# Attention over a K/V cache: cache rows of 16 KB, P transposed in 32x32 blocks, PV in diagonal 32x32 tiles

## The chip, the cores and the metric

The kernel runs on one core of a Trainium2 chip. The metric is the device time of one execution in microseconds (us). A profile of one execution comes beside the times: it records what every engine did and when. The engines are PE (TensorE, matmuls; PEld is its weight load, the stationary operand), DVE (VectorE), ACT (ScalarE), POOL (GpSimd) and SP (SyncE, which here issues the transfers from memory).

## The reference: what is computed

One attention block for 32 sequences (B) with 4 new tokens each, against a cache of 2048 positions. There are 32 query heads and 4 heads in the cache, so 8 query heads share one cache head g. All tensors are bf16.

```python
q = (x @ wq).reshape(B, 4, 32, 128).transpose(0, 2, 1, 3)      # x: [32, 4, 1024], wq: [1024, 4096]
k = repeat(k_cache, 8, axis=1)                                  # k_cache, v_cache: [32, 4, 2048, 128]
v = repeat(v_cache, 8, axis=1)
scores = einsum("bhqd,bhkd->bhqk", q, k) * 128 ** -0.5
p = softmax(scores, axis=-1)
o = einsum("bhqk,bhkd->bhqd", p, v)
out = o.transpose(0, 2, 1, 3).reshape(B, 4, 4096) @ wo          # wo: [4096, 1024]
```

The 8 query heads of one cache head times 4 tokens are 32 rows of scores. Four cache heads give 128 rows, so one sequence ("batch" below) fills the 128 partitions.

## The kernel before, in words

**Stages.** x is transposed on PE, Q^T is projected from wq (four loads of 2 MB, L209 to L229), then 32 batches run one after the other, and a last stage multiplies all 128 tokens by wo (L313 to L336, 64 matmuls of 512 columns at L318).

**Loads.** SP issues everything in one order: wq, K of three batches ahead, then V and K in turn, then wo. One load is 2 MB and takes one of nine slots of SBUF. A load waits until the slot's last user has read it (`freed`). K and V arrive as `g (p t) d -> p g (t d)` with p = 128 (L149): a partition gets 16 neighbouring cache positions of each of the four heads, which are four pieces of 4 KB.

**One batch on PE (L281 to L311, in program order).** `qk(i)`: 16 matmuls, QK^T into the four PSUM banks of `ps_s`, four 32-column tiles side by side (L285). `pv(i-1)`: 64 matmuls with a block of V (128x128) as the stationary operand and 32 columns of P^T moving (L267); they sum up O^T in `ps_o`. `kt_fill(i+2, f)`, f = 0 to 7: eight transposes each of K into a PSUM bank (L240). `tr_fill(i, f)`, f = 0 to 3: four matmuls each (L256) that transpose P with a diagonal matrix of 1/sum on the other side, so P^T comes out normalised.

**The ring.** K^T and P^T fills share four PSUM banks (`ps_a`, `ps_b`, `ps_c`, `ps_o`) in turn, and a fill waits until the bank's last fill was copied out (`ring_waits`). DVE and ACT share these copies: of the eight K^T copies ACT does f = 4, 6, 7 (`consumer`).

**The other engines per batch.** DVE: the maximum of each row (L379), the negated and scaled maximum (L380), the copy of O^T to `oT_sb` (L368), K^T copies (L353), 1/sum (L388), the diagonal matrix (L389), two P^T copies (L353). ACT: exp with the sum of each row (L408), then three K^T copies and two P^T copies (L355). Each engine takes its instructions in the order in which the program lists them, and waits where an instruction's semaphore is not there yet.

Of the kernel before, what the change touches and what calls it, by code (L numbers as in the profile page):

```python
# [54 lines left out]
def bass_standalone__gqa_block_cached__sampling_kernel(  # L55
# [17 lines left out]
    G = Hkv  # L73
    scale = float(Dh) ** -0.5
    NSLOT = 9
    SLOT = 8192
    NRING = 4
    KT_FILLS = 2 * G
    TR_FILLS = 4
    AHEAD = 2  # L80
    WQ_LOADS = 4
    WO_LOADS = 4
    HPL = Hq // WO_LOADS

# [5 lines left out]
    with ExitStack() as es:  # L90
        sb = lambda name, shape, dt: es.enter_context(nc.sbuf_tensor(name, shape, dt))
        slots = sb("slots", [128, NSLOT, SLOT], BF16)
        KT_sb = sb("KT_sb", [128, 2, G, Sk], BF16)
        QT_sb = sb("QT_sb", [128, B, Hq, Sq], BF16)
        oT_sb = sb("oT_sb", [128, Hq, NT], BF16)
        pp_sb = sb("pp_sb", [128, 2, Sk], BF16)
        ident = sb("ident", [128, 128], BF16)
        diag = sb("diag", [128, 2, 128], BF16)
# [4 lines left out]
        P_sb = pp_sb[:, 0, :]  # L103
        PT_sb = pp_sb[:, 1, :].rearrange("p (t r) -> p t r", r=128)
        x_sb = pp_sb[:, 0, 0:D]
        xT_sb = pp_sb[:, 0, D:2 * D].rearrange("p (a b) -> p a b", b=128)
        out_sb = pp_sb[:, 1, 0:D]

        ps_s = es.enter_context(nc.psum_tensor("ps_s", [128, Sk], F32))
        ring = [es.enter_context(nc.psum_tensor(f"ps_{c}", [128, 512], F32)) for c in "abco"]  # L110
        ring_f32 = [p[:, :] for p in ring]
        ring_bf16 = [p.bitcast(BF16) for p in ring_f32]
        ps_o = ring_f32[3]
# [3 lines left out]
        for n in ["x", "out"] + [f"slot{i}" for i in range(NSLOT)] + [f"wo{i}" for i in range(4)]:  # L117
            pr.sems[n] = es.enter_context(nc.semaphore(f"s_{n}"))
# [3 lines left out]
        for b in range(AHEAD + 1):  # L122
            stream.append(("k", b))
        for b in range(B):
            stream.append(("v", b))
            if b + AHEAD + 1 < B:
                stream.append(("k", b + AHEAD + 1))
# [13 lines left out]
        pr.load("sp", lambda e: e.dma_start(x_sb, x_flat[:, :]), "x", "x", 16)  # L141
        for n, l in enumerate(stream):
            kind, i = l
            waits = [freed(stream[n - NSLOT])] if n >= NSLOT else []
            s, v = f"slot{n % NSLOT}", 16 * (n // NSLOT + 1)
            if kind == "wq":
                fn = lambda e, l=l, i=i: e.dma_start(slot(l), wq_v[:, i, :])  # L147
            elif kind in "kv":
                src = (k_cache if kind == "k" else v_cache)[i].rearrange("g (p t) d -> p g (t d)", p=128)  # L149
                fn = lambda e, l=l, src=src: e.dma_start(slot(l).rearrange("p (g f) -> p g f", g=G), src)  # L150
            if kind != "wo":
                pr.load("sp", fn, l, s, v, waits)
                continue
            last = i == WO_LOADS - 1
            parts = 4 if last else 1
            per = HPL // parts
            for q in range(parts):
                fn = lambda e, l=l, i=i, q=q, per=per: e.dma_start(
                    slot(l)[:, q * per * D:(q + 1) * per * D].rearrange("p (h n) -> p h n", n=D),
                    wo_v[:, i * HPL + q * per:i * HPL + (q + 1) * per, :],  # L160
                )
                if last:
                    pr.load("sp", fn, ("wo", i, q), f"wo{q}", 16, waits)
                else:
                    pr.load("sp", fn, l, s, v, waits)
# [3 lines left out]

        jobs = [("kt", b, f) for b in range(AHEAD) for f in range(KT_FILLS)]  # L170
        for i in range(B):
            if i + AHEAD < B:
                jobs += [("kt", i + AHEAD, f) for f in range(KT_FILLS)]
            jobs += [("tr", i, f) for f in range(TR_FILLS)]
        job_index = {j: n for n, j in enumerate(jobs)}

        def consumer(job):
            kind, _, f = job
            if kind == "kt":
                return "act" if f in (4, 6, 7) else "dve"  # L180
            return "dve" if f in (0, 2) else "act"

        def ring_waits(job):
            n = job_index[job]
            if n < NRING:
                return [("q_evac", n)]
            w = [("evac",) + jobs[n - NRING]]
            if n % NRING == 3:
                b = job[1] - AHEAD - 1 if job[0] == "kt" else job[1] - 1
                if b >= 0:  # L190
                    w.append(("ot", b))
            return w


        pr.op("pool", lambda e: e.memset(ident[:], 0.0), [], "zero")
        pr.op("pool", lambda e: e.affine_select(
            out=ident[:], in_=ident[:], compare_op=ALU.not_equal, fill=1.0, base=0,
            pattern=[[-1, 128]], channel_multiplier=1), ["zero"], "ident")
# [33 lines left out]
        def kt_fill(b, f):  # L232
            job = ("kt", b, f)
            dst = ring_bf16[job_index[job] % NRING]
            g, half = f // 2, f % 2

            def fn(e):
                for q in range(8):
                    t = half * 8 + q
                    ins = e.transpose(  # L240
                        dst[:, q * 128:(q + 1) * 128],
                        slot(("k", b))[:, (g * NKT + t) * Dh:(g * NKT + t + 1) * Dh],
                        ident[:, :],
                    )
                return ins

            pr.op("pe", fn, [("k", b)] + ring_waits(job), job)

        def tr_fill(b, f):
            job = ("tr", b, f)  # L250
            dst = ring_f32[job_index[job] % NRING]

            def fn(e):
                for q in range(4):
                    t = f * 4 + q
                    ins = e.matmul(dst[:, q * 128:(q + 1) * 128], lhsT=P_sb[:, t * 128:(t + 1) * 128],  # L256
                                   rhs=diag[:, b % 2, :], start=True, stop=True)
                return ins

            pr.op("pe", fn, [("exp", b), ("diag", b)] + ring_waits(job), job)  # L260

        def pv(b):
            def fn(e):
                v = slot(("v", b))
                for g in range(G):
                    for t in range(NKT):
                        ins = e.matmul(  # L267
                            ps_o[:, 32 * g:32 * (g + 1)],
                            lhsT=v[:, (g * NKT + t) * Dh:(g * NKT + t + 1) * Dh],
                            rhs=PT_sb[:, t, 32 * g:32 * (g + 1)],  # L270
                            start=(t == 0),
                            stop=(t == NKT - 1),
                        )
                return ins

            w = [("v", b)] + [("evac", "tr", b, f) for f in range(TR_FILLS)]
            if b > 0:
                w.append(("ot", b - 1))
            pr.op("pe", fn, w, ("pv", b))

        def qk(i):  # L281
            def fn(e):
                for c in range(Sk // 512):
                    for g in range(G):
# [3 lines left out]
                            rhs=KT_sb[:, i % 2, g, c * 512:(c + 1) * 512],  # L288
# [4 lines left out]
                return ins  # L293

            w = [("evac", "kt", i, f) for f in range(KT_FILLS)]
            w += [("q_evac", j) for j in range(NB)] if i == 0 else [("exp", i - 1)]
            pr.op("pe", fn, w, ("qk", i))
# [4 lines left out]
        for i in range(B):  # L302
            qk(i)
            if i >= 1:
                pv(i - 1)
# [165 lines left out]
```

## Time and profile before

| what | value |
|---|---|
| time, median of 3 runs | 389.67 us (389.29 to 390.6) |
| the profiled execution's own time | 388.88 us |
| its span, from the first to the last instruction | 386.9 us |
| busy: PE, PEld, DVE, ACT | 296.0, 246.8, 242.4, 196.6 us |
| moved by DMA | 152.26 MB, mean 393 GB/s |

A row of the profile's groups gives source line, engine, operation, the tensors out<-in, shapes and count; then the busy time, the mean duration of one in ns, the idle time of the engine before it and what ended that. A timeline row gives start, length, engine, line and count of instructions that ran in a row. Matmuls overlap, so the mean of one is longer than the step from one to the next.

### The profile page before, as it was taken

What the parts mean: (1) busy time and instruction counts of PE and PEld (TensorE: products, weight loads), DVE (VectorE), ACT (ScalarE), POOL (GpSimd) and SP (SyncE); (2) the same over time, 40 slices, a digit from 0 to 9 for tenths busy, and PEclk for the clock granted to TensorE, in tenths of its full rate; (3) what the DMA queues carried; (4) which work ended last, traced back from release to release, by engine and by line L of the source; (5) the groups of instructions that cost most, each with busy time, mean ns of one, the idle gap of its engine ahead of it and who ended that gap; (6) DMA issues with size and microseconds to landing.
All of it is one profiled execution on the core that took longest, in us unless ns stands there. A gap on an engine that the chain in (4) does not pass through costs nothing.

```text
span 386.9 us, 11667 instructions
## 1 busy us (share of the span) xinstructions
PE 296.0 (77%) x5448; PEld 246.8 (64%) x5448; DVE 242.4 (63%) x390; ACT 196.6 (51%) x230; POOL 0.7 (0%) x6
## 2 busy tenths in 40 slices
PE   2877787776977977878788869877777787886596
PEld 1777576665766766767667657666666677664542
DVE  0026787775777777758777757877777577774400
ACT  1024766652655565466564635666555564664300
POOL 0000000000000000000000000000000000000000
PEclk9999999998999899889898979999999898997689
DMA  8999999999999999999999999999999999999981
GB/s 327 430 412 410 407 404 407 408 408 409 406 406 409 407 409 410 406 409 407 407 409 409 405 410 410 405 409 408 407 407 407 408 409 407 409 408 359 372 327 56
DMA packets 38912, 152.26 MB, mean 393 GB/s; under 512 B 1232, under 2 KB 1232, under 8 KB 38352
## 3 DMA queue, kind: packets, MB, share of 16 engines
q1 hardware_dynamic: 38864, 151.52, 98.5%
q8 instruction: 42, 0.69, 0.7%
q14 instruction: 6, 0.05, 0.0%
HBM read 151.26 MB, written 0.26 MB: 392 GB/s over the span
## 4 chain that ended last, share of the span: by engine, by line
DMA 87%; PE 7%; ACT 2%; DVE 2%; SPq 1%; issue 0%
DMA slots<-in_k_cache_dram 87%; PE ps_s L318 4%; DVE mx L379 1%; ACT pp_sb L408 1%; PE ps_s L285 1%; ACT KT_sb L355 1%; PE ps_a L240 1%; PE ps_o L267 0%; SPq L147 0%; PE ps_o L256 0%; PE ps_a L256 0%; PE ps_b L240 0%; SPq L150 0%; PE ps_c L256 0%; PE ps_b L256 0%
## 5 line engine op out<-in xcount | busy, mean ns | idle before, releaser
L408 ACT ACTIVATE pp_sb<-ps_s,negmx 128x2048 bf16<-128x2048 f32 x32 | 62.9, 1967 | 93.1 <-DVE negmx L380 93.1
L379 DVE TENSOR_REDUCE mx<-ps_s 128x1 f32<-128x2048 f32 x32 | 73.3, 2292 | 35.3 <-PE ps_s L285 35.3
L240 PE MATMUL ps_a<-ident,slots 128*128 128x128 bf16 x512 | 43.8, 234 | 42.2 <-DMA slots<-in_k_cache_dram 41.3
L240 PEld LDWEIGHTS ps_a<-ident,slots 128*128 128x128 bf16 x512 | 33.7, 105 | 46.1 <-DMA slots<-in_k_cache_dram 44.9
L267 PEld LDWEIGHTS ps_o<-pp_sb,slots 128*128 128x128 bf16 x2048 | 53.5, 96 | 14.6 <-issue 13.7
L267 PE MATMUL ps_o<-pp_sb,slots 128*128 128x32 bf16 x2048 | 56.7, 177 | 0.8 <-ACT pp_sb L355 0.8
L355 ACT ACTIVATE KT_sb<-ps_a 128x1024 bf16<-128x1024 bf16 x32 | 32.6, 1020 | 45.6 <-PE ps_a L240 45.6
L240 PE MATMUL ps_o<-ident,slots 128*128 128x128 bf16 x512 | 42.7, 231 | 7.8 <-DVE KT_sb L353 7.8
L353 DVE COPY KT_sb<-ps_b 128x1024 bf16<-128x1024 bf16 x64 | 43.7, 683 | 5.2 <-PE ps_b L240 5.2
L353 DVE COPY KT_sb<-ps_a 128x1024 bf16<-128x1024 bf16 x32 | 22.1, 689 | 35.0 <-PE ps_a L240 35.0
L240 PE MATMUL ps_c<-ident,slots 128*128 128x128 bf16 x512 | 43.3, 233 | 0.7 <-issue 0.7
L240 PE MATMUL ps_b<-ident,slots 128*128 128x128 bf16 x512 | 43.5, 234 | 0.0
L240 PEld LDWEIGHTS ps_o<-ident,slots 128*128 128x128 bf16 x512 | 33.8, 105 | 11.4 <-DVE KT_sb L353 11.2
L240 PEld LDWEIGHTS ps_c<-ident,slots 128*128 128x128 bf16 x512 | 34.8, 105 | 1.5 <-issue 0.9
L240 PEld LDWEIGHTS ps_b<-ident,slots 128*128 128x128 bf16 x512 | 35.2, 106 | 0.4
L285 PE MATMUL ps_s<-KT_sb,QT_sb 128*32 128x512 bf16 x512 | 34.3, 389 | 0.0
L355 ACT ACTIVATE KT_sb<-ps_c 128x1024 bf16<-128x1024 bf16 x32 | 32.7, 1021 | 1.9 <-PE ps_c L240 1.9
L355 ACT ACTIVATE KT_sb<-ps_o 128x1024 bf16<-128x1024 bf16 x32 | 32.9, 1027 | 0.0
L353 DVE CAST pp_sb<-ps_a 128x512 bf16<-128x512 f32 x32 | 22.1, 692 | 12.8 <-PE ps_a L256 12.8
L256 PE MATMUL ps_o<-diag,pp_sb 128*128 128x128 bf16 x128 | 13.2, 227 | 14.7 <-ACT KT_sb L355 14.7
L353 DVE CAST pp_sb<-ps_c 128x512 bf16<-128x512 f32 x32 | 21.9, 685 | 1.9 <-PE ps_c L256 1.6
L353 DVE COPY KT_sb<-ps_c 128x1024 bf16<-128x1024 bf16 x32 | 21.9, 684 | 1.0 <-PE ps_c L240 1.0
(46 smaller groups left out, 244.7 us busy)
## 6 DMA issues: line engine op xcount, KB each, us to landing
slots<-in_k_cache_dram SPq DMA_DIRECT2D x32, 2048.0 KB, 25.0
slots<-in_v_cache_dram SPq DMA_DIRECT2D x32, 2048.0 KB, 24.2
slots<-in_wq_dram SPq DMA_DIRECT2D x4, 2048.0 KB, 14.9
slots<-in_wo_dram SPq DMA_DIRECT2D x3, 2048.0 KB, 25.6
slots<-in_wo_dram SPq DMA_DIRECT2D x4, 512.0 KB, 12.2
pp_sb<-in_x_dram SPq DMA_DIRECT2D x1, 256.0 KB, 2.7
out_dram<-pp_sb SPq DMA_DIRECT2D x1, 256.0 KB, 2.2
```

The lines of the kernel that those rows point to most:

```text
L240: ins = e.transpose(dst[:, q * 128:(q + 1) * 128], slot(("k", b))[:, (g * NKT + t) * Dh:(g * NKT + t + 1) * Dh], ident[:, :],)
L256: ins = e.matmul(dst[:, q * 128:(q + 1) * 128], lhsT=P_sb[:, t * 128:(t + 1) * 128], rhs=diag[:, b % 2, :], start=True, stop=True)
L267: ins = e.matmul(ps_o[:, 32 * g:32 * (g + 1)], lhsT=v[:, (g * NKT + t) * Dh:(g * NKT + t + 1) * Dh], rhs=PT_sb[:, t, 32 * g:32 * (g + 1)], ...
L285: ins = e.matmul(ps_s[32 * g:32 * (g + 1), c * 512:(c + 1) * 512], lhsT=QT_sb[:, i, REP * g:REP * (g + 1), :], rhs=KT_sb[:, i % 2, g, c * ...
L318: ins = e.matmul(ps_s[:, c * 512:(c + 1) * 512], lhsT=oT_sb[:, h, :], rhs=w[:, h - i * HPL, c * 512:(c + 1) * 512], start=(h == 0), stop=( ...
L353: pr.op("dve", lambda e: e.tensor_copy(dst, src), w, ("evac",) + job)
L355: pr.op("act", lambda e: e.activation(dst, src, ACT.Copy), w, ("evac",) + job)
L379: pr.op("dve", lambda e, i=i: e.tensor_reduce(mx[:, i:i + 1], ps_s[:, :], AX.X, ALU.max), [("qk", i)], ("max", i))
L408: pr.op("act", lambda e, i=i: e.activation(P_sb, ps_s[:, :], ACT.Exp, bias=negmx[:, i:i + 1], scale=scale, accum_out=ssum[:, i:i + 1]), [( ...
```

## The change

The rows that a partition holds are other ones. K and V are now loaded as `g (p t) d -> (g p) (t d)` with p = 32: partition 32g+p holds 64 neighbouring positions of head g, one piece of 16 KB. The rest follows from this layout.

- K^T: transposing one of the 64 blocks gives 32 columns of each of the four heads, so `qk` takes its moving operand from K^T with a step between runs of 32 elements. It waits per pair of fills, in four parts.
- P^T: one DVE instruction transposes all of P in 32x32 blocks, SBUF to SBUF (L378), in place of 16 matmuls, four PSUM copies and the diagonal matrix. P^T has three buffers.
- PV: for each of the 64 positions t, four matmuls, one per head, each on 32 of the array's rows and 32 of its columns (`tile_position` 32g, 32g). P^T is stationary (32x32), V moves (32x128). Head g's sum stands in bank g of the ring, partitions 32g to 32g+31, so PV takes all four ring banks: it waits for the last copy out of each, and the next four fills wait for PV's results to be copied out (`pv`).
- The output: four ACT instructions of 32x128 scale it by 1/sum on the way to `o_sb` (L352), one PE transpose turns it (L247), one ACT copy takes it to `oT_sb` (L359).
- PV runs two batches behind QK (LAG 2, before 1), K is loaded four batches ahead (before 3), there are eight slots (before 9). ACT takes K^T fills 4 to 7, DVE 0 to 3. wo is loaded in 16 parts issued by POOL, after V of batch 30 has landed.

```diff
-    NSLOT = 9
+    NSLOT = 8
+    LAG = 2
...
-                src = (k_cache if kind == "k" else v_cache)[i].rearrange("g (p t) d -> p g (t d)", p=128)
+                src = v_cache[i].rearrange("g (p t) d -> (g p) (t d)", p=KP)
...
-                    pr.load("sp", fn, l, s, v, waits)
+                    pr.load("pool", fetch(part, wo_v[:, h0:h0 + WO_PER, :]), ("wo", i, q), f"wo{i * WO_PARTS + q}", 16, waits + [("v", B - 2)])
...
+        def take(job):
+            bank = turn[0] % NRING
+            turn[0] += 1
+            bank_of[job] = bank
+            before = bank_last[bank]
+            bank_last[bank] = ("evac",) + job
+            return bank, [before]
...
+        def o_fill(b):
+            job = ("o", b)
+            bank, waits = take(job)
+            dst = ring_bf16[bank]
+            pr.op("pe", lambda e: e.transpose(dst[:, 0:128], o_sb[:, b % 2, :], ident[:, :]), [("raw", b)] + waits, job)
+
+        def pv(b):
+            waits = list(bank_last.values())
+            for n in range(NRING):
+                bank_last[n] = ("raw", b)
...
-                for g in range(G):
-                    for t in range(NKT):
+                for t in range(KTOK):
+                    for g in range(G):
                         ins = e.matmul(
-                            ps_o[:, 32 * g:32 * (g + 1)],
-                            lhsT=v[:, (g * NKT + t) * Dh:(g * NKT + t + 1) * Dh],
-                            rhs=PT_sb[:, t, 32 * g:32 * (g + 1)],
+                            pv_bank[g],
+                            lhsT=PT_buf[rows, b % NPT, t, :],
+                            rhs=v[rows, t, :],
...
+                            tile_position=(KP * g, KP * g),
...
+            pr.op("pe", fn, [("v", b), ("pt", b)] + waits, ("pv", b))
...
         for i in range(B):
             qk(i)
-            if i >= 1:
-                pv(i - 1)
+            if i > LAG:
+                o_fill(i - 1 - LAG)
+            if i >= LAG:
+                pv(i - LAG)
             if i + AHEAD < B:
                 for f in range(KT_FILLS):
                     kt_fill(i + AHEAD, f)
-            for f in range(TR_FILLS):
-                tr_fill(i, f)
...
+        def raw_evac(b):
+            for g in range(G):
+                rows = slice(KP * g, KP * (g + 1))
+                w = [("pv", b), ("rinv", b)] + ([("o", b - 2)] if b >= 2 else [])
+                pr.op("act", lambda e, g=g, rows=rows: e.activation(
+                    o_sb[rows, b % 2, :], pv_bank[g], ACT.Copy, scale=rinv[rows, b:b + 1]),
+                    w, ("raw", b) if g == G - 1 else None)
...
+            pr.op("dve", lambda e, i=i: e.transpose(PT_buf[:, i % NPT, :, :].rearrange("p t r -> p (t r)"), P_sb),
+                  [("exp", i)] + ([("pv", i - NPT)] if i >= NPT else []), ("pt", i))
```

The order in which PE gets its instructions, with what the first of each run waits for: one batch before. s_act, s_dve and s_slot0 are the semaphores that ACT, DVE and the load of a slot count up; `pp_sb` holds P and P^T.

```order
L285 MATMUL ps_s<-KT_sb,QT_sb 32x512 x16
L267 MATMUL ps_o<-pp_sb,slots 128x32 [waits s_act,s_dve,s_slot0]
L267 MATMUL ps_o<-pp_sb,slots 128x32 x63
L240 MATMUL ps_a<-ident,slots 128x128 [waits s_slot1]
L240 MATMUL ps_a<-ident,slots 128x128 x7
L240 MATMUL ps_b<-ident,slots 128x128 x8
L240 MATMUL ps_c<-ident,slots 128x128 x8
L240 MATMUL ps_o<-ident,slots 128x128 [waits s_dve]
```

The same place of the changed program; `ps_r` is the whole ring.

```order
L275 MATMUL ps_s<-KT_sb,QT_sb 32x512 [waits s_act]
L275 MATMUL ps_s<-KT_sb,QT_sb 32x512 x15
L247 MATMUL ps_r<-ident,o_sb 128x128 [waits s_act]
L259 MATMUL ps_r<-slots,PT_sb 32x128 [waits s_act,s_slot2]
L259 MATMUL ps_r<-slots,PT_sb 32x128 x255
L233 MATMUL ps_r<-ident,slots 128x128 [waits s_act,s_slot3]
L233 MATMUL ps_r<-ident,slots 128x128 x31
L233 MATMUL ps_r<-ident,slots 128x128 [waits s_dve]
```

The K^T fills behind PV waited for their load alone; now the first of them waits for ACT as well (PV's results copied out), and PV itself waits for ACT's copy of the transposed output, which stands behind ACT's last K^T copy.

ACT's order, one batch before:

```order
L408 ACTIVATE pp_sb,ssum<-ps_s,negmx 128x2048
L355 ACTIVATE KT_sb<-ps_a 128x1024
L355 ACTIVATE KT_sb<-ps_c 128x1024
L355 ACTIVATE KT_sb<-ps_o 128x1024
L355 ACTIVATE pp_sb<-ps_b 128x512
L355 ACTIVATE pp_sb<-ps_o 128x512
```

And now:

```order
L359 ACTIVATE oT_sb<-ps_r 128x32x4
L352 ACTIVATE o_sb<-ps_r,rinv 32x128 x4
L393 ACTIVATE P_sb,ssum<-ps_s,negmx 128x2048
L338 ACTIVATE KT_sb<-ps_r 128x1024 x4
```

ACT's exp stood ahead of the K^T copies and behind nothing of PV; now it stands behind the four scaled copies of PV's result.

234 lines of the change are left out of this document (95 added, 139 removed).

## The prediction

> **What bounds the kernel now.** I read the page first: the span, the chain that ended last, and the bandwidth in 40 slices.
>
> ```profile
> span 386.9 us, 11667 instructions
> ...
> GB/s 327 430 412 410 407 404 407 408 408 409 406 406 409 407 409 410 406 409 407 407 409 409 405 410 410 405 409 408 407 407 407 408 409 407 409 408 359 372 327 56
> ...
> DMA 87%; PE 7%; ACT 2%; DVE 2%; SPq 1%; issue 0%
> ```
>
> The chain is 87% DMA, and the bandwidth stands at 404 to 412 GB/s from the third slice to the 36th: the transfers run without a break while K and V are loaded. A batch is 4.19 MB (two loads of 2.097 MB), which at 408 GB/s takes 10.28 us, and 32 of them 329 us.
>
> Next the waits (us in total, times, the longest): do the engines wait for transfers?
>
> ```profile
> PE ps_a L240 <- DMA slots<-in_k_cache_dram: 41.3, 30, 3.4
> ```
>
> In 30 of the batches PE waits for its next K, 1.4 us each. So PE is ahead of the transfers, by little: what counts is how much serial work the change puts into one batch, set against 10.28 us.
>
> The speed of the transfers by stretch (time, PE, PEld, DVE, ACT, POOL busy, clock, DMA share, GB/s): wq, whose rows are 16 KB already, then K and V in 4 KB, then wo.
>
> ```profile
> 5.00:20.00 15.00, 8.87 (x130) 8.70 (x131) 0.30 (x1) 0.00 (x0) 0.00 (x0) 1.00 0.99 421
> ...
> 200.00:210.00 10.00, 7.66 (x137) 6.64 (x138) 6.61 (x10) 5.06 (x7) 0.00 (x0) 0.83 1.02 408
> ...
> 365.00:375.00 10.00, 8.75 (x95) 4.68 (x93) 0.92 (x2) 0.70 (x2) 0.00 (x0) 0.74 1.00 373
> ```
>
> With 16 KB pieces a batch would take 4.19 MB / 421 = 9.96 us, at the 430 of the second slice 9.75 us. That is the whole gain that the new rows can bring, 0.3 to 0.5 us a batch, and only while transfers are what is waited for.
>
> **The change: one round of a batch.** In the program's order PE runs qk(i), the transpose of O(i-3), pv(i-2), then eight K^T fills. PV now takes all four ring banks. So the round closes on itself: PV waits for the last K^T copies out of the ring (ACT's f = 4 to 7) and for ACT's O copy behind them; the next fills wait for ACT's four scaled copies of PV's result; ACT's exp stands behind those; ACT's K^T copies stand behind exp. Before, PV only needed `ps_o` and ran beside the others' copies. I add up this ring, counted from PV's last matmul. First two durations of ACT, from the groups by shape (busy us, mean ns of one, idle before):
>
> ```profile
> L355 ACT ACTIVATE KT_sb<-ps_c 128x1024 bf16<-128x1024 bf16 x32 | 32.7, 1021 | 1.9 <-PE ps_c L240 1.9
> ...
> L355 ACT ACTIVATE pp_sb<-ps_b 128x512 bf16<-128x512 f32 x32 | 19.4, 607 | 3.4 <-PE ps_b L256 3.4
> ```
>
> Then steps between neighbours, from the timeline of one batch: DVE and ACT copies, K^T fills at full clock, and the softmax of a batch.
>
> ```profile
> 196.94 0.61 PE L240 MATMUL ps_b<-ident,slots 128*128 128x128 bf16 x8
> ...
> 197.39 0.61 PE L240 MATMUL ps_c<-ident,slots 128*128 128x128 bf16 x8
> ```
>
> ```profile
> 198.99 1.01 ACT L355 ACTIVATE KT_sb<-ps_a 128x1024 bf16<-128x1024 bf16 x1
> 199.49 0.68 DVE L353 COPY KT_sb<-ps_o 128x1024 bf16<-128x1024 bf16 x1
> 199.90 1.02 ACT L355 ACTIVATE KT_sb<-ps_c 128x1024 bf16<-128x1024 bf16 x1
> 200.09 0.68 DVE L353 COPY KT_sb<-ps_b 128x1024 bf16<-128x1024 bf16 x1
> ...
> 202.30 1.05 PE L285 MATMUL ps_s<-KT_sb,QT_sb 128*32 128x512 bf16 x16
> ...
> 203.40 2.29 DVE L379 TENSOR_REDUCE mx<-ps_s 128x1 f32<-128x2048 f32 x1 [0.99 <-PE ps_s L285]
> ...
> 205.72 0.15 DVE L380 TENSOR_SCALAR negmx<-mx 128x1 f32<-128x1 f32 x1
> ...
> 205.91 1.97 ACT L408 ACTIVATE pp_sb<-ps_s,negmx 128x2048 bf16<-128x2048 f32 x1 [2.91 <-DVE negmx L380]
> ...
> 207.78 0.19 ACT L408 ACTIVATION_READ_ACCUMULATOR pp_sb<-ps_s,negmx 128x1 f32 x1
> ```
>
> A fill of eight transposes starts 0.45 us after the one before, so 56 ns a transpose, and ends 0.61 us after its start. ACT copies start 0.91 us apart, DVE copies 0.60. Exp with its accumulator is 2.06 to 2.16 us.
>
> Scaled copy, 32x128: no row has it. A line through 512 (0.607) and 1024 (1.021) gives 0.81 ns an element and 0.19 us fixed, so 0.30 us for 128. Exp (1.97 for 2048) lies 0.11 us above that line and has an operand per partition, as the scaled copy has, which would make 0.41. I take 0.38, near the row with such an operand, and 0.10 of overlap with the next, as ACT's copies have it: 3 x 0.28 + 0.38 = 1.2 us. At least it is 3 x 0.20 + 0.30 = 0.9.
>
> From PV's end: scaled copies until 1.25 (with 0.05 for the signal). PE's fills start at 1.3, the first four in free banks; the fifth starts at 3.1 (DVE has emptied its bank at 1.9 + 0.7 = 2.6) and is done at 3.75. ACT's exp ends at 3.4, hidden. ACT's four K^T copies: 3.8 + 3 x 0.92 + 1.02 = 7.6. O copy, 0.30 less 0.10 overlap, and 0.1 for the signal to PE: 7.9. PE's last fill (DVE's fourth copy ends 4.5, fill until 5.2), qk (1.05) and the transpose of O end by 6.8, inside this; so does DVE (copies to 4.5, P's block transpose, maximum). The block transpose has no row: a bf16 copy of 2048 elements would be 2 x 0.68 = 1.4 us, the maximum over 2048 takes 2.29, twice that is 4.6. I take 2.3; even 4.6 ends at 9.3 and the next maximum at 11.7, ahead of the next exp. So **a round is 7.9 us + P**, with P the time of PV.
>
> **P.** 256 matmuls of 128 columns on 32x32 tiles, four heads in turn; no row has these. The nearest is QK's: four tiles of 32 columns side by side. A window that ends at 202.40, and the whole of it:
>
> ```profile
> 202.30 0.40 PE L285 MATMUL ps_s<-KT_sb,QT_sb 128*32 128x512 bf16 x4
> ```
>
> ```profile
> L285 PE MATMUL ps_s<-KT_sb,QT_sb x16: 378/379/390, 202.3 to 203.0; 128*32 128x512 bf16 x16
> ```
>
> Four start within 0.1 us though each lasts 0.38, and four sets of four take 1.05 us: the tiles run together, at 0.22 us a set of 512 columns. For 128 columns a set is then 54 ns by this row (0.215 / 4), 56 by the fills. P = 64 x 56 ns + 0.22 (a matmul's own length less its step) = 3.8 us; at least 3.65. The other end is the fastest that matmuls have followed each other for long, old PV:
>
> ```profile
> L267 PE MATMUL ps_o<-pp_sb,slots x64: 176/176/189, 203.3 to 204.9; 128*128 128x32 bf16 x64
> ```
>
> From the first start at 203.3 to the last at 204.9 are 63 steps of 25 ns, with 32 columns each. If that is what any matmul with its weight load needs to get in, P = 256 x 25 ns + 0.2 = 6.6 us. [...] I take 3.8, since QK has the tiles side by side as the new PV does.
>
> So a round is 11.7 us, over the 10.28 of before and the 9.96 of faster transfers: DMA waits for slots from then on, and its gain is worth nothing. The eight slots hide this: four rounds are 47 us, and a load takes 25.
>
> **Head.**
>
> ```profile
> 29.92 0.62 PE L240 MATMUL ps_a<-ident,slots 128*128 128x128 bf16 x8 [1.35 <-DMA slots<-in_k_cache_dram]
> ```
>
> Up to K of batch 0 nothing changes (wq bounds it): 29.9. K of batch 1 lands 5 us later, its fills end 38.5, qk 39.6. Two softmax rounds without PV follow: maximum 2.44 (with the scaling), exp 2.16, then DVE's rest of copies and 1/sum 0.5, block transpose 2.3; again 2.44, exp 2.16; four ACT copies 3.8: the first PV starts at 55.4. K and V are there by 50.
>
> **Tail.** PV of batches 0 to 27 is followed by fills; PV of batch 28 starts at 55.4 + 28 x 11.7 = 383. From there, one after the other: PV 3.8, scaled 1.25, exp 2.16, qk and O 1.8 (9.0); PV, 1.25, exp 2.16, O copy 0.3 (16.6); PV, 1.25, O turned and copied 0.7 (22.4); PV, 1.25, 0.7 (28.2). wo, 8.4 MB at 373 GB/s in 22.5 us, is loaded meanwhile: its last slot comes free with the fills of batch 31, 2.7 us ahead of this PV. Without that cover it would cost up to 22 us; behind the POOL queue's waits stands nothing else. The last stage is as before:
>
> ```profile
> 368.45 14.86 PE L318 MATMUL ps_s<-slots,oT_sb 128*128 128x512 bf16 x64 [0.47 <-DVE oT_sb L368]
> ```
>
> 386.9 - 368.45 = 18.4 us to the end of the span. **Sum**: 55.4 + 28 x 11.7 + 28.2 + 18.4 = 430 us of span, and 388.88 - 386.9 = 2 us around it: 432 us. The profiled run stood 0.8 us under the median, which changes nothing here. P enters 32 times, the ring's 7.9 us 28 times. A 0.3% step (1.2 us, about what a measurement of this kernel can tell from no change) is far off.
>
> **Rivals.** *DMA stays the bound, faster*: if a round came under 10.28 us, the 16 KB rows decide, 32 x 0.3 to 0.5 us less: 372 to 379, say 376 us. That needs P under 2.4 us, 37 ns a set; against it stand QK's set of 215 ns for 512 columns and the 7.9 us of each round in which PV can't run. 0.04; near equal, 0.01. *One at a time*: 25 ns a matmul, P = 6.6: 432 + 32 x 2.8 = 522. For it: no row shows matmuls fed faster than that for long. 0.28. *Half clock*: a waiting PE is granted half its clock:
>
> ```profile
> 228.68 1.03 PE L240 MATMUL ps_a<-ident,slots 128*128 128x128 bf16 x8 [3.19 <-DMA slots<-in_k_cache_dram]
> ...
> 229.50 1.06 PE L240 MATMUL ps_b<-ident,slots 128*128 128x128 bf16 x8
> ```
>
> Fills 0.82 apart instead of 0.45, after a wait of 3 us for K. In the new round PE idles 1.3 + 1.1 of 11.7 us, less at a stretch; if it happened throughout, P = 64 x 103 ns + 0.2 = 6.8, the eighth fill ends at 1.3 + 7 x 0.82 + 1.06 = 8.1, its copy and O's at 9.4, a round is 16.2: 432 + 28 x 4.5 + 4 x 3.0 = 570 us. 0.08. *Tiles one after the other*, each 56 ns: P = 14.5, 432 + 32 x 10.7 = 774. QK's row speaks against it. 0.04. That the rows aren't read as 16 KB would alter nothing, since transfers don't bind.
>
> **Numbers.** Forecast 432 with 0.55, then 0.28, 0.08, 0.04, 0.05. The range: down to 412 (scaled copies at 0.9, P at 3.65, and none of the 0.2 us that I put in for signals: 28 x 0.5 + 32 x 0.15 = 19), up to the one-at-a-time case, 525. Faster 0.04, same 0.01, slower 0.95.
>
> **What would show it.** Right: the chain of waits goes from DMA to ACT and PE; PV waits for ACT's O copy; the first fill waits for a scaled copy; rounds of 11.7 us; DMA idles, and K^T loads take longer from issue to landing than they need. P is read from PV's line: sets 56 ns apart, or matmuls 25 ns apart. Wrong: PE waiting for K as before, or a DVE transpose over 4.6 us that exp waits for.

## The result, and the profile after

The changed kernel takes 623.85 us (median of 4, 623.3 to 627.25) where the kernel before takes 389.55 (389.29 to 390.6): ratio 1.602, 95% interval 1.596 to 1.609. (Kernels below without an interval were run once.) The forecast was 432 us, range 412 to 525. The direction is right, the size is not: 192 us are missing from the sum. The profiled execution took 623.37 us, with a span of 621.4.

From the page of the kernel after: instructions by engine, the granted clock, the bandwidth, the packets that carry instructions (packets, MB, share), and the chain that ended last.

```profile
span 621.4 us, 23031 instructions
...
PE 392.4 (63%) x11110; PEld 341.5 (55%) x11112; DVE 240.0 (39%) x262; ACT 242.2 (39%) x358; POOL 12.3 (2%) x22
...
PEclk9999776788767788876778897786889886778799
...
GB/s 369 429 425 425 426 425 365 190 236 256 272 174 252 242 205 233 259 268 175 252 254 212 205 273 272 225 215 244 229 180 273 272 272 186 222 210 202 3 4 17
...
q8 instruction: 87, 1.43, 0.9%
...
PE 46%; ACT 27%; issue 20%; DMA 5%; DVE 2%; SPq 0%
```

Three things are as forecast. The chain has gone from DMA (87% before, 5% now) to PE and ACT. While slots are free, the new rows load at 425 to 429 GB/s, above the 404 to 412 of before. From the eighth slice on DMA waits for slots, and the bandwidth lies between 174 and 273. The new thing is "issue": 20% of the chain is time in which an engine waited for nothing that the profile shows. The waits name the engine (us in total, times, the longest):

```profile
PEld ps_r L259 <- issue: 162.8, 65, 4.6
PE ps_r L259 <- issue: 109.3, 31, 4.5
...
PE ps_r L233 <- ACT o_sb L352: 47.3, 28, 2.4
PE ps_r L259 <- ACT oT_sb L359: 39.8, 30, 1.6
```

The last two are the waits that the prediction named: the first fill for a scaled copy, PV for ACT's O copy. The first two were in no list of the prediction: PV stops inside itself, 31 times in 32 batches, 3.5 us each on average. One round in the timeline, from one PV's scaled copies to the next:

```profile
301.17 0.28 PE L259 MATMUL ps_r<-slots,PT_sb 32*32 32x128 bf16 x6 [3.07 <-issue]
...
301.50 1.47 ACT L352 ACTIVATE o_sb<-ps_r,rinv 32x128 bf16<-32x128 f32 x4 [7.23 <-PE ps_r L259]
...
303.11 6.42 PE L233 MATMUL ps_r<-ident,slots 128*128 128x128 bf16 x64 [1.66 <-ACT o_sb L352]
304.16 0.69 DVE L336 COPY KT_sb<-ps_r 128x1024 bf16<-128x1024 bf16 x1 [8.28 <-PE ps_r L233]
...
305.01 0.69 DVE L336 COPY KT_sb<-ps_r 128x1024 bf16<-128x1024 bf16 x1 [0.16 <-PE ps_r L233]
...
307.40 2.29 DVE L378 STREAM_TRANSPOSE PT_sb<-P_sb 128x2048 bf16<-128x2048 bf16 x1
307.57 3.77 ACT L338 ACTIVATE KT_sb<-ps_r 128x1024 bf16<-128x1024 bf16 x4 [2.52 <-PE ps_r L233]
...
309.46 1.05 PE L275 MATMUL ps_s<-KT_sb,QT_sb 128*32 128x512 bf16 x16
...
311.20 0.31 ACT L359 ACTIVATE oT_sb<-ps_r 128x128 bf16<-128x128 bf16 x1
...
311.66 2.52 PE L259 MATMUL ps_r<-slots,PT_sb 32*32 32x128 bf16 x168 [0.99 <-ACT oT_sb L359]
...
318.13 1.76 PE L259 MATMUL ps_r<-slots,PT_sb 32*32 32x128 bf16 x88 [3.95 <-issue]
...
319.94 1.47 ACT L352 ACTIVATE o_sb<-ps_r,rinv 32x128 bf16<-32x128 f32 x4 [8.42 <-PE ps_r L259]
```

The reader is to see two things. PV (the second of the two; of the first only the last six matmuls are in the window) runs 168 matmuls in 2.52 us, which is 41 steps of 56 ns and the 0.22 of a matmul's own length: exactly the forecast's speed. Then it stands 3.95 us and runs the other 88. And the 64 fills behind the first PV take 6.42 us (5.77 behind the second); DVE's first copies come 0.85 us apart, since they wait for fills that would start 0.45 apart at full clock. The round is 18.44 us, not 11.7.

The same engine further on, with the first and the last stage (PE's rows of the timeline):

```profile
54.75 2.47 PE L259 MATMUL ps_r<-slots,PT_sb 32*32 32x128 bf16 x164 [1.84 <-ACT KT_sb L338]
...
294.41 3.69 PE L259 MATMUL ps_r<-slots,PT_sb 32*32 32x128 bf16 x250 [0.90 <-ACT oT_sb L359]
...
330.11 3.19 PE L259 MATMUL ps_r<-slots,PT_sb 32*32 32x128 bf16 x214 [1.65 <-ACT oT_sb L359]
336.25 1.35 PE L259 MATMUL ps_r<-slots,PT_sb 32*32 32x128 bf16 x42 [2.96 <-issue]
...
347.50 2.28 PE L259 MATMUL ps_r<-slots,PT_sb 32*32 32x128 bf16 x132 [1.64 <-ACT oT_sb L359]
353.74 3.24 PE L259 MATMUL ps_r<-slots,PT_sb 32*32 32x128 bf16 x124 [3.96 <-issue]
...
564.08 2.58 PE L259 MATMUL ps_r<-slots,PT_sb 32*32 32x128 bf16 x172 [0.91 <-ACT oT_sb L359]
...
604.47 13.76 PE L312 MATMUL ps_s<-slots,oT_sb 128*128 128x512 bf16 x62 [0.67 <-ACT oT_sb L359]
```

The counts at which PV stops tell what it waits for. In four PVs in a row (294.41, 311.66, 330.11 and 347.50) they are 250, 168, 214 and 132. From one to the next the place moves by -82, +46 and -82 matmuls, that is by -164, +92, -164 instructions, since each matmul brings its weight load. -164 is 92 less 256. So the break returns at a fixed place in blocks of 256 instructions, whatever stands there. (A round has 674 matmuls and weight loads; the shift asks for two more, which the profile does not list: 676 + 92 is three blocks.) The page has these blocks too: 87 instruction packets of 1.43 MB / 87 = 16.4 KB, for 22222 instructions of PE, is one packet for 255. The kernel before, from its page:

```profile
PE 296.0 (77%) x5448; PEld 246.8 (64%) x5448; DVE 242.4 (63%) x390; ACT 196.6 (51%) x230; POOL 0.7 (0%) x6
...
q8 instruction: 42, 0.69, 0.7%
```

It has 10896 instructions on PE and 42 packets, one for 259. So PE's instructions come by DMA in blocks of 256, and a PV is two blocks, 512 instructions at 7 ns each. In each PV two borders are passed; the later one is where it stops (at 168, not at 40).

The trace has the time of every packet, so the break can be watched directly. What the DMA queues moved (q1 has K and V, q8 instructions; packets, MB, share) from the start of the PV at 311.66 to 315.8, and then in the one microsecond from 315.8 to 316.8:

```profile
q1 hardware_dynamic: 106, 1.74, 98.3%
```

```profile
q1 hardware_dynamic: 21, 0.10, 26.9%
q8 instruction: 1, 0.02, 5.9%
```

While the K load's packets run, no instruction packet comes; it comes among the load's last ones, at 315.82, is there at 316.76, and PE goes on at 318.13. Each of the 31 breaks ends 1.2 to 1.6 us after an instruction packet has arrived. In the 29 that fall beside loads, that packet starts 2.5 to 4.0 us after PE has passed the border before, and takes 0.9 to 1.1 us.

So the theory after the result: **instruction delivery**. PV uses up its instructions faster than they come, stands about 4 us (2.9 to 4.5 beside loads), and the fills behind most of these breaks are slow (25 of 28 rounds: 4.97 to 6.54 us for 64 transposes, the other three 3.80). The windows view of the kernel after shows the clock that PE was granted (the third number from the end) at 0.50 in the fills behind the PV of 311.66:

```profile
322.60:323.60 1.00, 1.00 (x12) 1.00 (x11) 0.83 (x2) 0.89 (x2) 0.00 (x0) 0.50 0.97 410
```

The rivals: the tiles themselves (32x32 in four places cost more than 56 ns a set in some way that shows as a break), and the ring of waits (which the order on ACT and DVE would cure).

### The profile page after: what moved, and what is told of

Same layout as the page of the kernel before. It is cut to its first block, busy times and chain, and to the rows that moved or that the text cites. A ratio compares the mean times of both kernels' runs of the same rounds, so it can differ in the third digit from the quotient of the medians.

```text
span 621.4 us, 23031 instructions
## 1 busy us (share of the span) xinstructions
PE 392.4 (63%) x11110; PEld 341.5 (55%) x11112; DVE 240.0 (39%) x262; ACT 242.2 (39%) x358; POOL 12.3 (2%) x22
## 3 DMA queue, kind: packets, MB, share of 16 engines
q8 instruction: 87, 1.43, 0.9%
## 4 chain that ended last, share of the span: by engine, by line
PE 46%; ACT 27%; issue 20%; DMA 5%; DVE 2%; SPq 0%
PE ps_r L259 24%; PE ps_r L233 19%; ACT KT_sb L338 18%; ACT o_sb L352 7%; DMA slots<-in_k_cache_dram 5%; PE ps_s L312 2%; ACT P_sb L393 1%; ACT oT_sb L359 1%; DVE mx L370 1%; PE ps_s L275 0%; DVE KT_sb L336 0%; SPq L156 0%; DVE PT_sb L378 0%; PE ps_r L247 0%; DVE PT_sb L380 0%
## 5 line engine op out<-in xcount | busy, mean ns | idle before, releaser
L259 PE MATMUL ps_r<-slots,PT_sb 32*32 32x128 bf16 x8192 | 149.4, 234 | 153.2 <-issue 109.3
L259 PEld LDWEIGHTS ps_r<-slots,PT_sb 32*32 32x32 bf16 x8192 | 137.1, 102 | 162.8 <-issue 162.8
L233 PE MATMUL ps_r<-ident,slots 128*128 128x128 bf16 x2048 | 174.4, 266 | 52.5 <-ACT o_sb L352 47.3
L233 PEld LDWEIGHTS ps_r<-ident,slots 128*128 128x128 bf16 x2048 | 167.9, 124 | 61.4 <-issue 53.6
L336 DVE COPY KT_sb<-ps_r 128x1024 bf16<-128x1024 bf16 x128 | 86.2, 689 | 295.1 <-PE ps_r L233 295.1
L352 ACT ACTIVATE o_sb<-ps_r,rinv 32x128 bf16<-32x128 f32 x128 | 45.9, 359 | 266.2 <-PE ps_r L259 264.9
L338 ACT ACTIVATE KT_sb<-ps_r 128x1024 bf16<-128x1024 bf16 x128 | 120.7, 1030 | 65.0 <-PE ps_r L233 65.0
L378 DVE STREAM_TRANSPOSE PT_sb<-P_sb 128x2048 bf16<-128x2048 bf16 x32 | 73.3, 2292 | 0.0
L393 ACT ACTIVATE P_sb<-ps_s,negmx 128x2048 bf16<-128x2048 f32 x32 | 62.9, 1967 | 3.2 <-DVE negmx L371 2.5
L312 PE MATMUL ps_s<-slots,oT_sb 128*128 128x512 bf16 x62 | 13.7, 379 | 0.7 <-ACT oT_sb L359 0.7
L247 PEld LDWEIGHTS ps_r<-ident,o_sb 128*128 128x128 bf16 x32 | 3.1, 96 | 17.9 <-ACT KT_sb L338 8.1
L377 DVE RECIPROCAL rinv<-ssum 128x1 f32<-128x1 f32 x32 | 4.9, 153 | 18.4 <-ACT P_sb L393 18.4
L359 ACT ACTIVATE oT_sb<-ps_r 128x128 bf16<-128x128 bf16 x32 | 9.8, 307 | 2.9 <-PE ps_r L247 2.9
```

What stands on the lines that cost most here:

```text
L233: ins = e.transpose(dst[:, q * 128:(q + 1) * 128], slot(("k", b))[:, t * Dh:(t + 1) * Dh], ident[:, :],)
L259: ins = e.matmul(pv_bank[g], lhsT=PT_buf[rows, b % NPT, t, :], rhs=v[rows, t, :], start=(t == 0), stop=(t == KTOK - 1), tile_position=(KP ...
L312: ins = e.matmul(ps_s[:, c * 512:(c + 1) * 512], lhsT=oT_sb[:, h, :], rhs=w[:, h - i * HPL, c * 512:(c + 1) * 512], start=(h == 0), stop=( ...
L336: pr.op("dve", lambda e: e.tensor_copy(dst, src), w, ("evac",) + job)
L338: pr.op("act", lambda e: e.activation(dst, src, ACT.Copy), w, ("evac",) + job)
L352: pr.op("act", lambda e, g=g, rows=rows: e.activation(o_sb[rows, b % 2, :], pv_bank[g], ACT.Copy, scale=rinv[rows, b:b + 1]), w, ("raw", b ...
```

## The experiments

**pv_full**: PV in whole-array matmuls of the same columns, a quarter of the instructions.

```diff
-                    for g in range(G):
-                        rows = slice(KP * g, KP * (g + 1))
...
-                            lhsT=PT_buf[rows, b % NPT, t, :],
-                            rhs=v[rows, t, :],
+                        lhsT=PT_buf[:, b % NPT, 4 * (t % 16):4 * (t % 16) + 4, :],
+                        rhs=v[:, t, :],
```

> The changed kernel, with PV as 64 matmuls on the whole array (P^T block 128x128 stationary, V 128x128 moving, one PSUM bank) in place of 256 on 32x32 tiles. It leaves the separation of the heads out: heads and positions are summed in a wrong way, but as many columns stream through the array (64 x 128 in a row) and everything around PV stays. Theory F (PE's instructions arrive too slowly: 512 of them for one PV, the break stands at the same count modulo 256): 128 instructions a PV, no break inside PV, K^T fills back at 0.45 us each, a round of about 12.0 us, about 440 us in all. Rival T (the break belongs to what PV does in the array and PSUM, not to the count): PV still 8 us, about 620 us.

Measured: 440.38 us, span 438.4. PE's timeline, one round, and the page's instruction packets:

```profile
221.48 3.73 PE L257 MATMUL ps_r<-slots,PT_sb 128*128 128x128 bf16 x64 [1.57 <-ACT oT_sb L356]
226.87 3.81 PE L233 MATMUL ps_r<-ident,slots 128*128 128x128 bf16 x64 [1.65 <-ACT o_sb L349]
...
233.39 3.73 PE L257 MATMUL ps_r<-slots,PT_sb 128*128 128x128 bf16 x64 [1.57 <-ACT oT_sb L356]
```

```profile
q8 instruction: 39, 0.64, 0.6%
```

63 steps of 56 ns and 0.22 without a break, fills at full clock (1.00 in the windows view from 200 to 300 us), a round of 11.91 us where the prediction has 11.7. The ring of waits stands near the forecast; the missing time goes with PV's 512 instructions on tiles. This alone doesn't part instructions from tiles.

**pv_half**, **pv_n32**, **pv_wide** keep the tiles. pv_half leaves out every second position (128 matmuls); pv_n32 keeps 256 matmuls with 32 columns in place of 128; pv_wide keeps 256 with 512 columns.

```diff
-                for t in range(KTOK):
+                for t in range(0, KTOK, 2):
```

> The changed kernel, with every second of the 64 positions left out of PV: 128 matmuls on 32x32 tiles, still four side by side. It leaves half of the attention's weighted sum out. Theory F: 256 instructions in one go instead of 512, 418 a round instead of 674; the break is gone or well under 4 us, PV 2 to 4 us, a round of 10.2 to 13 us, 385 to 470 us in all. Rival T (the break comes with the tiles, whatever their number): PV 8.3 - 1.8 = 6.5 us, the fills slow as now, about 565 us.

```diff
-                            pv_bank[g],
+                            pv_bank[g][:, KP * (t % 4):KP * (t % 4 + 1)],
...
-                            rhs=v[rows, t, :],
+                            rhs=v[rows, t, KP * (t % 4):KP * (t % 4 + 1)],
```

> The changed kernel, with 32 columns of V per matmul instead of 128 (each of the four column blocks gets a quarter of the positions): it leaves three quarters of the weighted sum out, with the same 256 matmuls on the same tiles in the same banks. Theory F: the count of instructions is as before, so PV stays near 8 us, the break only gets longer by the streaming that is saved: 590 to 625 us. Rival T (array time and a fixed break): streaming falls from 3.6 to 1.0 to 1.6 us, 540 to 560 us.

```diff
-                            pv_bank[g],
+                            ring_f32[g][rows, :],
...
-                            rhs=v[rows, t, :],
+                            rhs=slot(("v", b))[rows, 512 * (t % 16):512 * (t % 16 + 1)],
```

> The changed kernel with 512 columns moving in each of PV's 256 matmuls instead of 128 (four positions beside each other, only the first 128 columns are read, so the sums are wrong). Same count of instructions, four times the streaming: 64 sets of 215 ns, 13.8 us, 27 ns per instruction instead of 7. Theory F (a rate: 256 instructions take longer to come than the array needs for them): no break, PV 14 us, a round of 8.2 + 14 = 22.2 us, 55 + 28 x 22.2 + 4 x 14 + 49 = some 780 us, or 820 with slow fills. Rival C (a fixed break for each 256 instructions, whatever the pace): PV 18 us, over 900 us.

Measured: 450.94, 599.68 and 767.94 us. PE's timeline of pv_half, of pv_n32 and of pv_wide:

```profile
202.90 2.11 PE L233 MATMUL ps_r<-ident,slots 128*128 128x128 bf16 x35 [0.93 <-issue]
...
220.63 1.97 PE L259 MATMUL ps_r<-slots,PT_sb 32*32 32x128 bf16 x128 [1.64 <-ACT oT_sb L359]
```

```profile
215.09 1.73 PE L259 MATMUL ps_r<-slots,PT_sb 32*32 32x32 bf16 x194 [1.64 <-ACT oT_sb L359]
221.31 0.67 PE L259 MATMUL ps_r<-slots,PT_sb 32*32 32x32 bf16 x62 [4.49 <-issue]
```

```profile
298.51 13.99 PE L259 MATMUL ps_r<-slots,PT_sb 32*32 32x512 bf16 x256 [1.57 <-ACT oT_sb L359]
314.17 3.80 PE L233 MATMUL ps_r<-ident,slots 128*128 128x128 bf16 x64 [1.67 <-ACT o_sb L352]
```

With half of the tiles most PVs run through (1.97 us is 31 steps of 56 ns and 0.22); a break still comes at times, nine in PV and nine in the fills. They and the slow fills (5.50 us at 212.35, where those at 224.27 took 3.81) are not cheap: a round without any is 10.15 us here (11.91 of pv_full less the 1.76 by which PV is shorter), and the mean of 28 is 12.51. A quarter of the columns brings little, 24 us of 624: PE reaches the border sooner (194 matmuls in 1.73 us, so about 9 ns each) and stands longer, and from PV's start to its restart it is 6.2 us (215.09 to 221.31) where it was 6.5 in the kernel after (311.66 to 318.13). Four times the columns take the break away, with all 512 instructions in place, because they then pass at 27 ns each: a block of 256 lasts 7.0 us instead of 1.8. All three times are where theory F put them (767.94 a little under its 780). Tiles and counts are not what breaks; the rate of instructions is.

**quiet**: the changed kernel, with the later K and V loads cut to 512 B for each partition.

```diff
-                pr.load("sp", fetch(slot(l), src), l, s, v, waits)
+                w = SLOT if n < NSLOT + WQ_LOADS else 256
+                pr.load("sp", fetch(slot(l)[:, 0:w], src[:, 0:w]), l, s, v, waits)
```

> The changed kernel with all but the first K and V loads cut to 512 bytes per partition (later batches compute on what is left in the slots): nearly no traffic beside the instructions' own. Theory L (the time until the next 256 instructions are there is their own): the break stays at 3.5 to 4.2 us, 590 to 620 us. Rival C (instruction packets queue behind K and V on the DMA engines): the break shrinks under 2 us, the fills keep their clock more often, under 560 us.

Measured: 513.79 us, span 511.8. PE's timeline:

```profile
214.91 2.40 PE L261 MATMUL ps_r<-slots,PT_sb 32*32 32x128 bf16 x158 [1.57 <-ACT oT_sb L361]
218.68 1.57 PE L261 MATMUL ps_r<-slots,PT_sb 32*32 32x128 bf16 x98 [1.37 <-issue]
221.91 3.81 PE L235 MATMUL ps_r<-ident,slots 128*128 128x128 bf16 x64 [1.66 <-ACT o_sb L354]
...
228.43 3.03 PE L261 MATMUL ps_r<-slots,PT_sb 32*32 32x128 bf16 x204 [1.57 <-ACT oT_sb L361]
232.48 0.91 PE L261 MATMUL ps_r<-slots,PT_sb 32*32 32x128 bf16 x52 [1.02 <-issue]
```

The break shrinks from 4 us to 1.0 to 1.4 (0.95 to 1.7 over the 26 breaks between the full loads at either end), so the rival of this run holds. Not one instruction was taken away. The fills behind it take 3.81 us, as at full clock, in 17 of 28 rounds (kernel after: 3 of 28); the first round shown is 13.52 us, the mean of 28 is 14.27. The packets' times say where the break shrinks: an instruction packet now starts 0.5 to 1.1 us after PE has passed the border before, instead of 2.5 to 4.0. The rest is much as before: 0.9 to 1.5 us to arrive, 1.2 to 1.6 more until PE goes on. So a block takes 3.0 to 3.5 us from the border to PE by itself, while PV uses one up in 1.8; beside K and V its packet starts some 2.7 us later. That it queues behind them on the DMA engines fits all of this; the queue itself isn't seen.

**ring_order**, **full_ring_order**, **full_dve6** test the ring. The first two put exp ahead of the scaled copies on ACT and give ACT every second fill, in the changed kernel and in pv_full. The third is pv_full with six K^T copies on DVE and two on ACT.

```diff
-        ACT_FILLS = (4, 5, 6, 7)
+        ACT_FILLS = (1, 3, 5, 7)
...
-            if i >= LAG:
-                raw_evac(i - LAG)
             pr.op("act", lambda e, i=i: e.activation(
...
+            if i >= LAG:
+                raw_evac(i - LAG)
```

> The changed kernel, with two things moved on ACT and DVE: exp(i) stands ahead of the four scaled copies, and ACT takes the odd K^T fills and DVE the even ones. Theory F (PE's instruction fetch breaks PV and the half clock after it slows the fills): PV and fills stay as they are, the fills at 0.85 us each set the pace of the copies, so 610 to 630 us. Rival R (the ring of waits is what costs): the round loses over 1 us, under 590 us.

> The same two moves in the kernel whose PV is 64 matmuls on the whole array (heads and positions summed in a wrong way). There no break hides the ring: copies of ACT and DVE alternate, exp runs beside PV, PV starts 7.1 us after the last one's end instead of 8.2. Theory (once the break is gone, the ring of waits sets the round): 28 x 1.1 us off 440 us, 405 to 415 us. Rival (what is left is not the ring): 440 us.

```diff
-        ACT_FILLS = (4, 5, 6, 7)
+        ACT_FILLS = (5, 7)
```

> The kernel whose PV is 64 matmuls on the whole array (heads and positions summed in a wrong way), with DVE taking six of the eight K^T copies and ACT only f = 5 and 7; the order of exp and scaled copies stays as in the changed kernel. DVE's own work is 9 us a batch. Theory (the ring of waits sets the round once the break is gone): the copies are out of the ring 6.2 us after PV's end, qk, O's transpose and its copy at 6.9, a round of 10.8 us instead of 11.9: 440 - 28 x 1.1 = 409 us. Rival (what is left is not the ring): 440 us.

Measured: 606.31, 491.35 and 409.92 us. The first lies between the two ranges that were expected for it, nearer to theory F's. The second is a miss, and slower than pv_full. Its waits, and the fills of one round:

```profile
ACT P_sb L388 <- DVE negmx L368: 110.4, 32, 3.5
...
PE ps_r L233 <- ACT o_sb L349: 88.5, 28, 3.2
```

```profile
230.14 5.13 PE L233 MATMUL ps_r<-ident,slots 128*128 128x128 bf16 x64 [3.19 <-ACT o_sb L349]
```

I had exp's wait for the maximum hidden. It is not: the maximum stands behind the block transpose on DVE, exp waits 3.5 us for it, the scaled copies now stand behind exp, and PE's fills wait 3.2 us for these where they waited 1.66. After that wait the first fills come 0.85 us apart (the copies behind them start at 231.19, 232.04 and 232.89), and all eight take 5.13 us instead of 3.81, with no break of instructions at all: behind a wait of 3.2 us stands here what stands behind the breaks, and behind the 1.66 of pv_full it does not. full_dve6 gives what was expected of it: with the break gone, four ACT copies of 0.92 us set the round, and two fewer take 30 us off. In the changed kernel the two moves of ring_order bought 17 us of 624: the breaks stay (36 of them, 120.5 us in its waits), so the ring is the smaller part there.

**rows16_only**: the kernel before with 16 KB rows for K and V and nothing else.

```diff
-                src = (k_cache if kind == "k" else v_cache)[i].rearrange("g (p t) d -> p g (t d)", p=128)
+                src = (k_cache if kind == "k" else v_cache)[i].rearrange("g (p t) d -> (g p) (t d)", p=128 // G)
```

> The kernel before, with only the source of its K and V loads changed to one piece of 16 KB per partition: it computes with heads and positions in wrong places, at the same work for every engine. Theory: transfers bound it and 16 KB pieces move at 421 to 430 GB/s, so 372 to 379 us. Rival (the engines' own round is no shorter than 10.2 us, or the pieces' size is not what holds 408 GB/s): no change, 389 us.

Measured: 377.41 us (375.49 to 378.31) against 388.46, ratio 0.970 (0.965 to 0.975). Ten of its microseconds in the windows view (as in the prediction, GB/s last):

```profile
200.00:210.00 10.00, 9.26 (x167) 8.17 (x165) 7.34 (x10) 4.84 (x7) 0.00 (x0) 0.84 1.00 421
```

The gain that the layout itself brings is real: 11 us, within the 372 to 379 us that the prediction gave for faster rows alone.

**k16_v4**, **k16_vorder**, **k16_qk** try to keep half of it: K alone in 16 KB pieces, the whole reference computed, V and PV as before. Tokens then come out in another order than V's, and it must be mended somewhere: by exp writing P with 8 B between neighbours; by V loaded in four DMAs of 32 partitions, in the order of K, with exp writing runs of 64 B; by QK reading K^T with 4 KB between neighbours. The diffs show this mending alone: in all three, K's load, its fills and its copies are changed as in the changed kernel.

```diff
-                P_sb, ps_s[:, :], ACT.Exp, ...
+                P_sb.rearrange("r (t k c) -> r c t k", t=16, k=32, c=4),
```

> The kernel before with K alone in pieces of 16 KB (partition 32g+p, 64 positions), V in pieces of 4 KB as before; QK's moving operand steps between runs of 32 elements, and exp writes P in V's order, 8 bytes between neighbours. It computes the whole reference. Theory: K moves at 425 GB/s and V at 408, 0.21 us a batch less, 382 us beside 388.5. Rival: exp's scattered output or the stepped operand takes longer and the engines' round passes 10.1 us: 388 us or more.

```diff
-                    src = v_cache[i].rearrange("g (p t) d -> p g (t d)", p=128)
+                src = v_cache[i].rearrange("g (k c t) d -> c k g (t d)", k=32, c=4)
+                for c in range(4):
...
+                        slot(l)[32 * c:32 * (c + 1), :].rearrange("p (g f) -> p g f", g=G), src[c])
```

> The kernel before with K alone in pieces of 16 KB, V in pieces of 4 KB loaded by four DMAs per batch whose partition order (32c+k) suits K's, and exp writing P in runs of 32 elements (64 bytes). It computes the whole reference. Theory (it was exp's scattered output that cost 2.85 us a batch in the other order; runs of 64 bytes cost nothing): exp back at 2.0 us, K at 425 GB/s, V at 408, 382 us beside 389. Rival: V's loads of 32 partitions are slower, or exp still is: 389 us or more.

```diff
-                            rhs=KT_sb[:, i % 2, g, c * 512:(c + 1) * 512],
+                            rhs=KT_sb[:, i % 2, :, g, :].rearrange("d (c t) k -> d t k c", c=4)[:, 4 * c:4 * c + 4],
```

> The kernel before with K alone in 16 KB pieces and the whole reference computed; V stays in 4 KB. The order of the tokens is mended where QK reads K^T as its moving operand: neighbouring columns then lie 4 KB apart in a partition, and the scores come out in V's order, so exp writes contiguously and V's load is untouched. Theory L (the layout gain is real and only its mending cost us in the two earlier tries): QK stays at 389 ns a matmul, K is loaded at the faster rate, about half of the 11 us that both rows brought: 382 to 385 us. Rival S (PE reads far-apart columns more slowly): QK takes twice its 1.05 us or more; PE had 1.4 us to spare in a batch, so at twice 385 to 390, at four times (3.2 us more, 1.8 over the spare) 389 + 32 x 1.8 = 447 us.

All three are slower. k16_v4: 467.61 us, ratio 1.200 (1.197 to 1.204). k16_vorder: 630.57, 1.615 (1.610 to 1.619). k16_qk: 427.79, 1.100 (1.098 to 1.102). The price of each, in order: exp by group; the waits, and the windows view; QK by group, and the sixteen of one batch in the timeline.

```profile
L409 ACT ACTIVATE pp_sb<-ps_s,negmx 128x2048 bf16<-128x2048 f32 x32 | 154.1, 4814 | 112.8 <-DVE negmx L381 112.8
```

```profile
PE ps_a L250 <- DMA slots<-in_k_cache_dram: 210.3, 32, 8.8
```

```profile
200.00:210.00 10.00, 6.23 (x76) 5.89 (x76) 4.45 (x9) 2.50 (x3) 0.00 (x0) 0.65 1.02 246
```

```profile
L287 PE MATMUL ps_s<-KT_sb,QT_sb 128*32 128x512 bf16 x512 | 115.9, 1036 | 0.0
```

```profile
210.08 3.62 PE L287 MATMUL ps_s<-KT_sb,QT_sb 128*32 128x512 bf16 x16
```

In k16_v4 exp takes 4.81 us instead of 1.97. In k16_vorder, V's loads of 32 partitions come with transfers of 246 GB/s in place of 408, and PE waits 6.6 us for every K. In k16_qk the matmuls of QK take 3.62 us a batch instead of 1.05, and one 1036 ns instead of 389. The first two expectations missed; of the third, the rival that far-apart columns are read slowly is right (at 3.4 times the 1.05 us, 428 us). No version that computes the whole reference was found that beats the kernel before.

## Why the prediction was wrong, step by step

The sum's terms against the quoted timeline (a round is the mean of 28, from PV of batch 0 at 54.75 to PV of batch 28 at 564.08):

| term | forecast, us | measured, us | difference |
|---|---|---|---|
| to the first PV | 55.4 | 54.75 | -0.7 |
| 28 rounds | 28 x 11.7 | 28 x 18.19 | +181.7 |
| PV of batch 28 to the last stage | 28.2 | 40.4 | +12.2 |
| last stage | 18.4 | 16.9 | -1.5 |

- **The step that failed** is "P = 64 x 56 ns + 0.22 = 3.8 us". The 56 ns a set are right (168 matmuls in 2.52 us; pv_wide's 13.99 us are the 0.215 us a set of QK's row). Left out was that 512 instructions must be there to run so: their delivery was put at nothing, without a reason. In the round shown P is 8.3 us (311.66 to 319.94): 3.8, a break of 3.95, and a slower end. pv_full and pv_wide, each without the break, quiet, with a smaller one, and the instruction packet that comes before each restart show this cause.
- **The ring, 7.9 us**, is 10.2 in the round shown (301.50 to 311.66) and 8.2 in pv_full (11.91 less 3.73). Scaled copies took 1.47 (forecast 1.2, the 0.3 that pv_full's ring is longer); from ACT's first K^T copy to PV it is 4.1, as forecast. The other 2 us are the fills at half clock, up to the fifth (granted clock 0.55 from 303.11 to 309.40). So the half-clock rival was half right: it named the fills' 0.82 us apart, for waits of another kind. That it goes with the break is shown by pv_full, where all fills behind PV take 3.81 us, and quiet, where most do; in full_ring_order it comes behind a wait of 3.2 us with no break. The length of a wait alone doesn't decide it, as the rival had it: in the kernel before, the clock was 0.50 in the fills behind a wait of 1.66 us for K (at 206.70) and 1.00 in those behind 1.80 us (at 70.82), and three rounds of fills in the kernel after kept their 3.80 us behind breaks of 4.0 to 4.2 us, with over 100 matmuls of PV in between (others with as many did not). What decides it, no run shows.
- **pv_full's 440 us** is near the forecast's sum (432): its rounds are 0.2 us longer than forecast, 28 times, and its tail (388.16 to 421.27, 33.1 us) 4.9 longer. It stands for the kernel with a quarter of PV's instructions. The 183 us of span from there to the kernel after (621.4 against 438.4) come with the instruction stream, breaks and half clock together; 110 of them go when K and V hardly move (quiet: 511.8).
- **One at a time** (25 ns a matmul, from old PV's row; 522 us) did not happen: four tiles go in 56 ns. 168 matmuls in 2.52 us are 15 ns each, and with 32 columns it is 9 (pv_n32: 194 in 1.73 us). The rival pointed at the right risk, a price for each instruction, by another mechanism.
- **DMA** went as said: faster rows, no value past 10.28 us a round. The block transpose was taken at 2.3 and took 2.29. Of the tail's +12.2 us, 4.9 stand in pv_full too, without a break: there PE waits 3.65 us for exp, and the last three PVs take 5.0 to 5.4 us instead of 3.73. So the tail, too, was a little short by itself; the rest is PV's break of 4.46 us at 566.66 and smaller ones.
- **The range** held only prices for each matmul by itself. The supply of instructions had no row in the profile of before, but had a trace: 42 instruction packets, one for 259 instructions. Twice the instructions of PE, and those of PV at 7 ns each where the old PV's came at 12.5 (25 ns for a matmul and its weight load), should have asked what brings them.

What stays open: why a packet starts 2.5 to 4.0 us after the border beside K and V, what the 1.2 to 1.6 us after its arrival are, and how far ahead of PE a block can be fetched, which no run shows. From PV's start to its restart it is 6.1 to 8.2 us over the 29 PVs, so neither a fixed time from the border nor from PV's start fits exactly.

## What to carry to other kernels

Count instructions as a resource beside time: here a burst of 512 at 7 ns each outran its supply, and beside bulk transfers the wait was some three times as long (2.9 to 4.5 us instead of quiet's 0.95 to 1.7); matmuls of 512 columns hid it (pv_wide, 27 ns an instruction), those of 128 or 32 on the same tiles didn't. This layout cut the contraction to a quarter and paid with four times the instructions (512 a PV, pv_full 128), so price a layout with everything that it forces (the new order cost 39 to 241 us where it was mended elsewhere, against a gain of 11 for both rows). And when an accumulator takes over a ring that others use, add up the ring first: here that sum was right to 0.3 us once the break was gone, and already meant slower.

## What the runs showed of the hardware that I had not expected

- In the kernel after, PE's instructions came by DMA in packets of 16.4 KB, one for about 255 instructions (87 for 22222). At the 31 breaks PE went on 1.2 to 1.6 us after a packet's arrival; the breaks were 2.9 to 4.5 us beside K and V, and in quiet, beside almost no traffic, 0.95 to 1.7.
- Exp that writes 2-byte elements 8 B apart took 4814 ns for 128x2048 instead of 1967 (k16_v4); in runs of 64 B (k16_vorder) it kept 1967.
- A moving operand with neighbours 4 KB apart took PE 3.4 times as long (k16_qk, sixteen QK matmuls of 512 columns: 3.62 us instead of 1.05); in runs of 64 B it took 1.05 (the kernel after).
- Four DMAs of 32 partitions for each V, in 4 KB pieces and beside 16 KB ones, brought the whole core from 408 to 246 GB/s (k16_vorder, 200 to 210 us).
- Behind a wait of 3.2 us PE's next 64 transposes took 5.13 us (full_ring_order), behind one of 1.66 us 3.81 (pv_full). The granted clock behind a wait of 1.66 us in the kernel before was 0.50, behind one of 1.80 us 1.00.
